# Ninth chunk's attention in four array quarters, and the last two tiles' stores merged, in a linear-attention-plus-MLP kernel

## Chip, cores and metric

The kernel runs on one core of one Trainium2 chip. The metric is the device time of one execution in microseconds (us). A core has these engines: TensorE (PE, with its weight loads shown apart as PEld), VectorE (DVE), ScalarE (ACT), GpSimd (POOL) and SyncE (SP). SP, ACT and POOL also issue DMA transfers. TensorE writes into PSUM, which has eight banks; VectorE and ScalarE read it from there.

## The reference

Inputs are q, k and v of shape (8, 8, 576, 64): batch, heads, sequence, head width. All inputs and the output are float32.

```python
q_s = softmax(q, axis=-1)                       # over the 64 features
k_s = softmax(k, axis=2)                        # over the sequence
kv = np.einsum('bhsd,bhse->bhde', k_s, v)       # 64 x 64 per head
attn = np.einsum('bhsd,bhde->bhse', q_s, kv)
x = attn.transpose(0, 2, 1, 3).reshape(8, 576, 512)
xn = (x - mean(x)) / sqrt(var(x) + 1e-6) * g_ln
out = x + relu(xn @ w_ch1) @ w_ch2              # 512 -> 2048 -> 512
```

## The kernel before

**Chunks and tiles.** The 576 rows of each batch are cut into 512 and 64. The 512 rows are a chunk of 4 tiles of 128 rows, so there are eight chunks, 0 to 7, one for each batch. The eight remainders of 64 rows make a ninth chunk, `C9`: its tile `t` holds in partitions 0 to 63 the remainder of batch `2t`, in partitions 64 to 127 that of batch `2t + 1`.

**Attention of a chunk.** For each pair of heads `i` (4 pairs of 2 x 64 = 128 features), `kv_sb[:, b, i, :]` holds a 128x128 block with the two heads' 64x64 matrices on its diagonal and zeros elsewhere. `po_mm` (line 380) multiplies the transposed exponentials of q, `eqTs`, with it. For chunks 0 to 7 that is one matmul per tile and pair, over the full array (line 387). For the ninth chunk (line 394) the two halves of a tile belong to different batches, so each pair takes two matmuls: 128 rows of the array (both heads), 64 columns (the 64 tokens of one batch), and 128 streamed columns of that batch's block, half of whose products are with zeros. The two matmuls write partitions 0 to 63 and 64 to 127 of the same bank. A tile `po` (128 x 512 float32) fills one PSUM bank and comes from the pool `att_ps`, which has two banks; so tile 0 takes the first, tile 1 the second, tile 2 the first again and tile 3 the second again.

**After it.** `x_fast` (line 424) reads a bank on VectorE: one `scalar_tensor_tensor` (line 427) scales by the reciprocals of the softmax sums (`eqs[c][2]`, one for each head) and adds up the row (`accum_out`) into `mv[:, t, 0:1]`. `xn_out` (line 419) then centres the row. `square_sum` (line 407, ScalarE) adds up the squares. `xn_T` (line 267) transposes two tiles at a time by a DMA on SP's queue, and `sum_x` (line 259) makes the sums of transposed blocks that the next product needs.

**The MLP of a chunk.** Both products are done by a seven-product (Strassen-like) scheme. `mm1_fast` (line 714; matmuls of line 711, outputs `bx`, `bb`, `bc`) makes the hidden layer `hT`. `mm2_fast` (line 644; matmuls of line 566, banks `ba`, `bb`, `bc`, `be`) does the second product. VectorE (lines 550, 594, 742, 745) and ScalarE (lines 591, 666, 735, 739, 753) form the sums between the products. Line 577 makes the output tiles of chunks 1 to 7.

**What sets the order.** The program is written out by hand, in order, for every engine (`manual_schedule`). `run` (line 798) walks through a chunk's matmuls, each with a weight of 0.5, and puts the side work in where the running sum of weights passes a given number. While chunk 7's MLP runs, `attn_rest` (line 870) makes the ninth chunk's attention: tiles 0 and 1 at 14, their reads at 22 and 54, tiles 2 and 3 at 58, their reads at 66 and 75. Squares are at 46, 62, 69 and 77, the transposes at 61 and 78. So each engine meets this work at a fixed place in its queue.

**The end.** The last chunk's second product is `last_products` (line 596). Its outputs lie in one tile `yl`; `stt` (line 606, VectorE) writes one 128x256 half of one tile. `store` (line 611) issues two DMAs, partitions 0 to 63 from SP's queue and 64 to 127 from ACT's (line 616). There are five calls, so ten DMAs: three of two tiles (128 KB each) and two of one tile (64 KB each). After them SP waits for every DMA queue's semaphore, one by one (line 1147), and the program ends.

Of the kernel before, what the change touches and what calls it, by code (L numbers as in the profile page):

```python
# [12 lines left out]
FP32 = mybir.dt.float32  # L13
BF16 = mybir.dt.bfloat16
AF = mybir.ActivationFunctionType
ALU = mybir.AluOpType
# [4 lines left out]
def kernel(  # L21
# [16 lines left out]
    nc = tc.nc  # L38

    B, H, S, D = q.shape  # L40
    DM = H * D
    DH = 4 * DM
    P = 128
# [5 lines left out]
    NP = H // 2  # L49
# [3 lines left out]
    C9 = B  # L53
# [15 lines left out]
    att_ps = ctx.enter_context(tc.tile_pool(name="att_ps", bufs=2, space=PS))  # L69
# [19 lines left out]
    kv_sb = const.tile([P, B, NP, P], BF16)  # L89
# [85 lines left out]
    eks, eqs, eqTs, xs, xnTs, rstds, tqs = {}, {}, {}, {}, {}, {}, {}  # L175
# [165 lines left out]
    halves = (slice(0, 64), slice(64, P))  # L341
# [36 lines left out]
    pobox = {}  # L378

    def po_mm(c, t, i):  # L380


        if i == 0:
            pool, tag = (mm_ps, "m") if c == 0 and t >= 2 else (att_ps, "a")
            pobox["p"] = pobox[c, t] = pool.tile([P, DM], FP32, tag=tag, name="po")
        if c < B:
            nc.tensor.matmul(  # L387
                pobox["p"][:, i * P : i * P + P], eqTs[c][:, t, i, :], kv_sb[:, c, i, :],
                start=True, stop=True,
            )  # L390
        else:
            for half in range(2):
                ps = slice(64 * half, 64 * half + 64)
                nc.tensor.matmul(
                    pobox["p"][ps, i * P : i * P + P], eqTs[c][:, t, i, ps],
                    kv_sb[:, 2 * t + half, i, :], start=True, stop=True,
                )

    def stats(c, t, src):
        _, st, _, mv = xs[c]  # L400
# [15 lines left out]
    def xn_out(c, t):  # L416

        x, _, xn, mv = xs[c]
        nc.vector.tensor_scalar(
            out=xn[:, t], in0=x[:, t], scalar1=float(DM), scalar2=mv[:, t, 0:1],  # L420
            op0=ALU.mult, op1=ALU.subtract,
        )

    def x_fast(c, t):

        x, st, _, mv = xs[c]
        nc.vector.scalar_tensor_tensor(  # L427
            x[:, t].rearrange("p (h d) -> p h d", h=H),
            in0=pobox[c, t].rearrange("p (h d) -> p h d", h=H), scalar=1.0,
            in1=eqs[c][2][:, t].to_broadcast([P, H, D]), op0=ALU.mult, op1=ALU.mult,  # L430
            accum_out=mv[:, t, 0:1] if c else st[:, t, 0:1],
        )
        if c:
            xn_out(c, t)
# [35 lines left out]
    hbox = {}  # L470
# [68 lines left out]
    def sum_h(g, i):  # L539

        if g == 0 and i == 0:
            hbox["s"] = mlp.tile([P, 4, KH, 2 * P], BF16, tag="hs", name="hs", bufs=1)
        ks = slice(KH // 2 * g, KH // 2 * g + KH // 2)
        s1, s2, s3, s4 = [hbox["s"][:, n, ks] for n in range(4)]
        a11, a12, a21, a22 = [h_part(odd, half, ks) for half in range(2) for odd in range(2)]
        dst, x, y, op = (
            (s1, a21, a22, ALU.add), (s2, s1, a11, ALU.subtract),
            (s3, a11, a21, ALU.subtract), (s4, a12, s2, ALU.subtract),
        )[i]
        nc.vector.tensor_tensor(out=dst, in0=x, in1=y, op=op)  # L550
# [18 lines left out]
    def bank(name):  # L569
        hbox[name] = mm_ps.tile([P, 2, DH2], FP32, tag="m", name="b" + name)  # L570
# [18 lines left out]
    def copy_u(name):  # L589
        hbox[name] = mlp.tile([P, 2, DH2], FP32, tag=name, name=name, bufs=1)  # L590
        nc.scalar.copy(hbox[name], hbox["a"])  # L591

    def add_u(dst, src):
        nc.vector.tensor_tensor(out=hbox[dst], in0=hbox["b"], in1=hbox[src], op=ALU.add)

    def last_products(product):

        c = C9
        yl = raw.tile([P, T, DM], FP32, tag="qt", name="yl")

        def part(t, col):
            return yl[:, t, DH2 * col : DH2 * col + DH2]

        def stt(t, col, src, add=None):
            cols = slice(DH2 * col, DH2 * col + DH2)
            nc.vector.scalar_tensor_tensor(
                part(t, col), in0=src, scalar=rstds[c][:, t : t + 1],
                in1=xs[c][0][:, t, cols] if add is None else add, op0=ALU.mult, op1=ALU.add,
            )

        def store(t0, tn, col):
            cols = slice(DH2 * col, DH2 * col + DH2)
            for half, eng in enumerate((nc.sync, nc.scalar)):
                ps = slice(64 * half, 64 * half + 64)
                to = out[2 * t0 + half : 2 * (t0 + tn) - 1 + half : 2, SM:S, cols]
                eng.dma_start(to.transpose([1, 0, 2]), yl[ps, t0 : t0 + tn, cols])

        def both(name, t0, col, add=False):
            for t in range(2):
                stt(t0 + t, col, hbox[name][:, t], part(t0 + t, col) if add else None)  # L620

        def own_bank():
            bank("d")

        def seed_e():
            bank("e")
            add_u("e", "s2")

        product(1, "a", first=True, cut=6, at={
            0: [lambda: sum_h(1, 0), lambda: sum_h(1, 1)],  # L630
            15: [lambda: both("a", 0, 0)]})
        product(2, "c", first=True, at={7: [lambda g=g: sum_h(g, 2) for g in range(2)],
            15: [lambda: both("c", 0, 0, True), lambda: store(0, 2, 0)]})
        product(6, "a", at={7: [lambda g=g: sum_h(g, 3) for g in range(2)], 15: [lambda: copy_u("s2")]})
        product(5, "b", first=True)
        product(7, "a", at={1: [seed_e, lambda: both("b", 2, 1)], 15: [
            lambda: both("a", 2, 1, True), lambda: stt(3, 0, hbox["a"][:, 1]),
            lambda: store(2, 2, 1)]})
        product(3, "e", at={15: [lambda: both("e", 0, 1), lambda: store(0, 2, 1), own_bank]})
        product(4, "a", ts=(0,), at={7: [lambda: stt(2, 0, hbox["a"][:, 0]), lambda: store(2, 1, 0)]})  # L640
        product(4, "d", ts=(1,), own=True, at={
            15: [lambda: stt(3, 0, hbox["d"][:, 1], part(3, 0)), lambda: store(3, 1, 0)]})

    def mm2_fast(c):

# [26 lines left out]
        if c == C9:  # L672
            last_products(product)
            return steps
# [154 lines left out]
    def attn_fast(c):  # L829

        s = [(4 + 4 * t, lambda t=t: reduce_q(3, t, 2)) for t in (0, 2)] if c == 3 else []
        kv, new, ps, squares, ts, rstd = (
            (24, 40, ((48, 53), (57, 59), (65, 67), (73, 75)), (66, 74, 87, 91), (61, 78), 95)
            if c == 3 else
            (3, 10, ((13, 24), (48, 53), (57, 59), (65, 67)), (60, 66, 74, 87), (55, 70), 92)
        )
        s += [(22 if c == 3 else 2, lambda: recip_q(c)), (kv, lambda: kv_pairs(c)), (new, lambda: start_x(c))]
        for t, (p0, p1) in enumerate(ps):
            s += spread([lambda t=t, i=i: po_mm(c, t, i) for i in range(NP)], p0, p1)
            s += [(p1, lambda t=t: x_fast(c, t)), (squares[t], lambda t=t: square_sum(c, t))]  # L840
        s += [(ts[0], lambda: xn_T(c, 0, 2)), (ts[1], lambda: xn_T(c, 2, 2)), (rstd, lambda: rstd_op(c))]
        s += [((84, 100 if c == C9 - 1 else 88, 92, 101)[i], lambda i=i: sum_x(c, i)) for i in range(4)]
        return s
# [26 lines left out]
    def attn_rest():  # L870

        s = [(2, lambda: recip_q(C9)), (4, lambda: start_x(C9))]
        for t, (p0, p1, p2) in enumerate(((14, 22, 46), (14, 54, 62), (58, 66, 69), (58, 75, 77))):
            s += [(p0, lambda t=t: [po_mm(C9, t, i) for i in range(NP)])]
            s += [(p1, lambda t=t: x_fast(C9, t)), (p2, lambda t=t: square_sum(C9, t))]
        s += [(61, lambda: xn_T(C9, 0, 2)), (78, lambda: xn_T(C9, 2, 2)), (88, lambda: rstd_op(C9))]
        return s + spread([lambda i=i: sum_x(C9, i) for i in range(4)], 102, 104)
# [274 lines left out]
```

## Time and profile before

| what | value |
|---|---|
| median of three runs | 264.89 us (264.72 to 265.26) |
| the profiled execution itself | 264.57 us |
| its span, first to last instruction | 262.8 us |
| granted TensorE clock, mean | 0.998 |
| line 394, ninth chunk's attention matmuls | 32, in two visits of 16, from 211.1 and 221.4 us |
| line 427, read of a 512-wide tile on VectorE | 0.68 us, and 0.08 us to read the accumulator |
| line 407, squares of a tile on ScalarE | 0.72 us, and 0.20 us to read the accumulator |
| last VectorE instruction (line 606) | starts at 258.45 us, takes 0.48 |
| end stores | 128 KB: 2.5 us (SP) and 2.8 us (ACT) from issue to landing |

A row of the timeline has the start (us from the start of the span), the time that the row covers, the engine, the line, the operation, what is written from what, the shape and the count; in brackets stands how long the engine had been idle before and what ended that. For matmuls the shape begins with the used part of the array (rows * columns), and a matmul's time is its whole way through the array, so matmuls overlap: their cost is read from the distances of their starts. A page line with shares of the chain follows the work back from the last instruction, at each step to what released it.

### The profile page before, as it was taken

How to read it: one execution, taken by the hardware profiler on the slowest of the kernel's cores; microseconds unless marked ns; L12 is line 12 of the kernel's file. 1: busy time of each engine (PE TensorE's matmuls, PEld its weight loads, DVE VectorE, ACT ScalarE, POOL GpSimd, SP SyncE). 2: the span in 40 equal slices, each digit the busy share in tenths (PEclk: the TensorE clock that was granted, in tenths of full speed). 3: DMA queues.
4: the chain of work that ended last, by engine and by line, in shares of the span. 5: the costliest groups of instructions: out<-in, count | busy, mean ns of one | idle time of the engine just before them, and what ended most of it. 6: DMA issues, size and time to landing. Idle time of an engine off the chain costs nothing.

```text
span 262.8 us, 6694 instructions
## 1 busy us (share of the span) xinstructions
PE 255.6 (97%) x2624; PEld 220.0 (84%) x2627; DVE 224.0 (85%) x492; ACT 174.3 (66%) x340; POOL 94.8 (36%) x148
## 2 busy tenths in 40 slices
PE   8999989999999999999999999999999999999993
PEld 6789745789888898999899889998899888888882
DVE  6879597999999999899889988998898869977872
ACT  4557780888977885789478947894788378447400
POOL 3962228233079104930980097009000800030000
PEclk9999999999999999999999999999999999999999
DMA  6999999979958995999299929994906320321014
GB/s 193 254 205 206 356 218 283 282 185 298 170 125 265 281 140 67 284 274 129 67 301 247 167 62 278 247 169 94 266 5 127 115 81 10 73 102 60 2 41 120
DMA packets 82536, 45.00 MB, mean 171 GB/s; under 512 B 58116, under 2 KB 79112, under 8 KB 82504
## 3 DMA queue, kind: packets, MB, share of 16 engines
q0 software_dynamic: 32464, 21.76, 44.2%
q1 hardware_dynamic: 49440, 22.29, 39.0%
q10 hardware_dynamic: 600, 0.53, 0.6%
q8 instruction: 20, 0.33, 0.5%
q14 instruction: 12, 0.10, 0.1%
HBM read 36.70 MB, written 9.44 MB: 176 GB/s over the span
## 4 chain that ended last, share of the span: by engine, by line
PE 82%; DMA 9%; POOL 3%; DVE 3%; ACT 1%; issue 0%; DVEq 0%
PE ba L566 21%; PE bx L711 20%; PE bb L711 10%; DMA qt<-in_q_dram 9%; PE be L566 5%; PE bc L566 5%; PE bb L566 5%; PE bc L711 5%; PE pc L519 3%; PE po L387 2%; PE pkv L357 2%; PE ph L483 1%; DVE x L427 1%; POOL w_raw L99 1%; DVE ot L500 1%; POOL v L965 1%
## 5 line engine op out<-in xcount | busy, mean ns | idle before, releaser
L566 PEld LDWEIGHTS <-hs 128*128 128x128 bf16 x512 | 49.8, 98 | 5.7
L711 PEld LDWEIGHTS <-w_q 128*128 128x128 bf16 x480 | 45.6, 98 | 5.1
L259 POOL TENSOR_TENSOR tq<-xnT 128x256 bf16<-128x256 bf16 x26 | 17.2, 677 | 77.0 <-DMA xnT<-xn 63.0
L566 PEld LDWEIGHTS <-hT 128*128 128x128 bf16 x384 | 37.1, 98 | 4.3
L711 PEld LDWEIGHTS <-w1g 128*128 128x128 bf16 x360 | 34.1, 98 | 4.1
L711 PE MATMUL bx<-tq,w_q 128*128 128x256 bf16 x240 | 31.7, 273 | 0.0
L566 PE MATMUL ba<-w_q,hs 128*128 128x256 bf16 x256 | 30.8, 273 | 0.0
L735 ACT COPY bc<-bx 128x512 f32<-128x512 f32 x30 | 16.7, 591 | 20.8 <-PE bx L711 20.5
L742 DVE TENSOR_TENSOR bb<-bx,s 128x512 f32<-128x512 f32 x30 | 19.5, 695 | 8.4 <-ACT s L739 5.7
L583 POOL DMA_DIRECT2D out_dram<-ot x28 | 15.4, 558 | 24.2 <-DVE ot L577 24.1
L427 DVE SCALAR_TENSOR_TENSOR x<-po,rq 128x512 bf16<-128x512 f32 x34 | 23.2, 683 | 0.9 <-PE po L387 0.7
L407 ACT ACTIVATE scrap<-x,mv 128x512 bf16<-128x512 bf16 x32 | 23.0, 720 | 1.4 <-DVE x L427 1.2
L753 ACT ACTIVATE hT<-bb 128x512 bf16<-128x512 f32 x30 | 16.3, 595 | 9.9 <-PE bb L711 9.1
L745 DVE TENSOR_TENSOR hT<-bx,s 128x512 bf16<-128x512 f32 x30 | 19.3, 684 | 3.8 <-PE bx L711 3.8
L387 PE MATMUL po<-kv_sb,eqT 128*128 128x128 bf16 x128 | 22.1, 219 | 0.0
L550 DVE TENSOR_TENSOR hs<-hT 128x1024 bf16<-128x1024 bf16 x32 | 21.6, 685 | 0.5 <-ACT hT L753 0.5
L753 ACT ACTIVATE hT<-bc 128x512 bf16<-128x512 f32 x30 | 16.4, 595 | 8.4 <-PE bc L711 8.4
L218 DVE TENSOR_REDUCE zq<-eq 128x16 f32<-128x1024 bf16 (+1 forms) x20 | 20.7, 1051 | 0.0
L591 ACT COPY s<-ba 128x512 f32<-128x512 f32 x15 | 8.7, 582 | 13.3 <-PE ba L566 8.6
L753 ACT ACTIVATE hT<-bx 128x512 bf16<-128x512 f32 x30 | 16.4, 604 | 0.7 <-PE bx L711 0.7
L566 PE MATMUL ba<-w_sb,hT 128*128 128x256 bf16 x128 | 16.7, 273 | 0.0
L739 ACT COPY s<-bb 128x512 f32<-128x512 f32 x30 | 16.5, 619 | 0.0
(152 smaller groups left out, 550.3 us busy)
## 6 DMA issues: line engine op xcount, KB each, us to landing
out_dram<-ot POOLq DMA_DIRECT2D x30, 256.0 KB, 5.0
qt<-in_q_dram SPq DMA_DIRECT2D x5, 1024.0 KB, 6.7
kt<-in_k_dram SPq DMA_DIRECT2D x5, 1024.0 KB, 12.2
qt<-in_q_dram POOLq DMA_DIRECT2D x2, 1024.0 KB, 12.4
kt<-in_k_dram POOLq DMA_DIRECT2D x2, 1024.0 KB, 14.1
vm<-in_v_dram POOLq DMA_DIRECT2D x16, 128.0 KB, 12.6
w_raw<-in_moe_w_ch_dram POOLq DMA_DIRECT2D x3, 512.0 KB, 10.4
w_sb<-in_moe_w_ch_dram POOLq DMA_DIRECT2D x3, 512.0 KB, 16.2
```

What stands on the lines that cost most here:

```text
L218: nc.vector.reduce_sum(eqs[c][1][:, ts], eqs[c][0][:, ts], axis=AX.X)
L259: eng.tensor_tensor(out=dst[:, t], in0=x[:, t], in1=y[:, t], op=ALU.subtract)
L387: nc.tensor.matmul(pobox["p"][:, i * P : i * P + P], eqTs[c][:, t, i, :], kv_sb[:, c, i, :], start=True, stop=True,)
L407: nc.scalar.activation(scrap, x[:, t], AF.Square, bias=mv[:, t, 0:1], scale=-float(DM), accum_out=mv[:, t, 1:2],)
L427: nc.vector.scalar_tensor_tensor(x[:, t].rearrange("p (h d) -> p h d", h=H), in0=pobox[c, t].rearrange("p (h d) -> p h d", h=H), scalar=1. ...
L550: nc.vector.tensor_tensor(out=dst, in0=x, in1=y, op=op)
L566: nc.tensor.matmul(hbox[bank][:, t], lhsT, rhs, start=first and (own or t == 0) and k == 0, stop=k == KH - 1, skip_group_check=True)
L711: nc.tensor.matmul(dst[:, q], lhsT, rhs, start=first and q == 0 and ko == 0, stop=ko == 1, skip_group_check=True)
L735: nc.scalar.copy(at[g, "c"], at[g, "x"])
L742: nc.vector.tensor_tensor(out=at[g, "b"], in0=at[g, "x"], in1=at[g, "s"], op=ALU.add)
L745: nc.vector.tensor_tensor(out=h_out(g, 1, 1), in0=at[g, "x"], in1=at[g, "s"], op=ALU.add)
L753: nc.scalar.activation(h_out(g, odd, half), at[g, name], AF.Relu)
```

## The change

For the ninth chunk, `po_mm` takes two banks for each pair of tiles (`t` = 0 and 1, then 2 and 3) and does four matmuls for each tile and pair of heads: batch `m` of the tile by head `half` of the pair. Each has 64 rows (one head's features), 64 columns (one batch's tokens) and 64 streamed columns (that head's 64x64 matrix). Rows 0 to 63 of the array (the first head) write the first bank, rows 64 to 127 (the second head) the second one. A visit (two tiles) is then 32 matmuls instead of 16. `x_fast` reads a tile with two `scalar_tensor_tensor` of 4 x 64 columns, one from each bank, with a row sum each, and a `tensor_add` of 128x1 joins the two sums. Chunks 0 to 7 keep their code. At the end, the store of tile 2's left half is left out, and the last call stores tiles 2 and 3 together: four calls, eight DMAs of 128 KB.

```diff
     def po_mm(c, t, i):
+        if c == C9:
+            if i == 0 and t % 2 == 0:
+                pobox["q"] = [
+                    att_ps.tile([P, 2, NP, D], FP32, tag="a", name="po") for _ in range(2)
+                ]
+            pobox[c, t] = pobox["q"]
+            for m, tok in enumerate(halves):
+                for half, hs in enumerate(halves):
+                    nc.tensor.matmul(
+                        pobox["q"][half][tok, t % 2, i, :], eqTs[c][hs, t, i, tok],
+                        kv_sb[hs, 2 * t + m, i, hs], start=(t % 2 == 0 and i == 0), stop=True,
+                        skip_group_check=True,
+                    )
+            return
         if i == 0:
             ...
-        if c < B:
-            nc.tensor.matmul(
-                pobox["p"][:, i * P : i * P + P], eqTs[c][:, t, i, :], kv_sb[:, c, i, :],
-                start=True, stop=True,
-            )
-        else:
-            for half in range(2):
-                ps = slice(64 * half, 64 * half + 64)
-                nc.tensor.matmul(
-                    pobox["p"][ps, i * P : i * P + P], eqTs[c][:, t, i, ps],
-                    kv_sb[:, 2 * t + half, i, :], start=True, stop=True,
-                )
+        nc.tensor.matmul(
+            pobox["p"][:, i * P : i * P + P], eqTs[c][:, t, i, :], kv_sb[:, c, i, :],
+            start=True, stop=True,
+        )
...
     def x_fast(c, t):
         x, st, _, mv = xs[c]
+        if c == C9:
+            for half in range(2):
+                nc.vector.scalar_tensor_tensor(
+                    x[:, t].rearrange("p (i two d) -> p i two d", two=2, d=D)[:, :, half],
+                    in0=pobox[c, t][half][:, t % 2], scalar=1.0,
+                    in1=eqs[c][2][:, t].rearrange("p (i two) -> p i two", two=2)[:, :, half]
+                    .to_broadcast([P, NP, D]),
+                    op0=ALU.mult, op1=ALU.mult, accum_out=st[:, t, half : half + 1],
+                )
+            nc.vector.tensor_add(mv[:, t, 0:1], st[:, t, 0:1], st[:, t, 1:2])
+            xn_out(c, t)
+            return
...
-        product(4, "a", ts=(0,), at={7: [lambda: stt(2, 0, hbox["a"][:, 0]), lambda: store(2, 1, 0)]})
+        product(4, "a", ts=(0,), at={7: [lambda: stt(2, 0, hbox["a"][:, 0])]})
         product(4, "d", ts=(1,), own=True, at={
-            15: [lambda: stt(3, 0, hbox["d"][:, 1], part(3, 0)), lambda: store(3, 1, 0)]})
+            15: [lambda: stt(3, 0, hbox["d"][:, 1], part(3, 0)), lambda: store(2, 2, 0)]})
```

## The prediction

> **What bounds the kernel now.** I read the page first: the busy shares, then the chain that ended last.
>
> ```profile
> PE 255.6 (97%) x2624; PEld 220.0 (84%) x2627; DVE 224.0 (85%) x492; ACT 174.3 (66%) x340; POOL 94.8 (36%) x148
> ...
> PE 82%; DMA 9%; POOL 3%; DVE 3%; ACT 1%; issue 0%; DVEq 0%
> ```
>
> TensorE (PE) is busy for 97% of the span, and it makes up 82% of the chain. Other engines matter where they hold PE up. The granted clock is 0.998, so no term below has a clock in it. Then I read the timeline around the two places where the ninth chunk's attention (line 394) stands.
>
> ```profile
> 210.62 0.60 PE L711 MATMUL bc<-xnT,w1g 128*128 128x256 bf16 x4
> 211.15 0.64 PE L394 MATMUL po<-kv_sb,eqT 128*64 128x128 bf16 x16
> 211.72 0.61 PE L711 MATMUL bc<-xnT,w1g 128*128 128x256 bf16 x4
> ```
>
> ```profile
> 220.71 0.68 DVE L427 SCALAR_TENSOR_TENSOR x<-po,rq 128x512 bf16<-128x512 f32 x1
> ...
> 221.32 0.08 DVE L427 DVE_READ_ACCUMULATOR x<-po,rq 128x1 f32 x1
> ...
> 221.43 0.64 PE L394 MATMUL po<-kv_sb,eqT 128*64 128x128 bf16 x16
> ```
>
> Full-array matmuls start 109 ns apart. The four at 210.62 leave PE free at 211.06, and the next of their kind starts at 211.72: a visit of line 394 costs 0.66 us. The second costs the same: four of line 566 start at 220.90, PE is free at 221.34, and the next starts at 222.00. Ahead of it DVE reads tile 1 from its bank, from 220.71 to 221.40; part 2 comes back to that. In the single records, 16 matmuls start as 8 pairs, 3 to 4 ns apart within a pair and 56 ns from pair to pair (80 before the second): 8 x 56 = 448 ns. The other 0.21 us is the way into the half array and back.
>
> **Part 1, the quarters.** Each visit's 16 matmuls of 128 rows x 64 columns (128 streamed) become 32 of 64 x 64 (64 streamed), with as many weight loads. Four in a row use four different quarters. If they run at once, a visit is 8 groups of four at a pitch P, plus the same 0.21 us. No row shows quarters. The nearest row for P is line 357, two half-array tiles with 65 streamed columns:
>
> ```profile
> 182.53 0.32 PE L357 MATMUL pkv<-vm,ek 128*64 128x65 bf16 x8
> ...
> 183.16 0.20 PE L357 MATMUL pkv<-vr,ekr 128*64 128x65 bf16 x2
> 183.29 0.39 PE L711 MATMUL bx<-xnT,w1g 128*128 128x256 bf16 x2
> ```
>
> Its 40 matmuls are 20 pairs. The first starts at 182.53, the last at 183.16: 0.63 / 19 = 33 ns a pair, and 32 without the slower first step. That visit costs 0.85 us, 20 x 32 = 0.64 and again 0.21, so the cost of going in and out does not hang on the count. I take P = 32: 64 streamed columns instead of 65, and the partner tiles ride 4 ns behind. That is 256 ns against 448, **0.19 us less a visit, 0.38 for two**. Bounds for P: 29 ns, the shorter steps of line 357, gives 0.43; above, a group that splits into two pairs, 64 ns, costs 0.13 for two visits, and four matmuls one by one are the second rival. I take the low end because halves side by side already overlap in this trace.
>
> **Part 2, the banks, a wait that is added.** Before, tiles 0 to 3 alternated between two banks, and only the 9th matmul of the second visit (tile 3, at 221.68) needed the read of tile 1, over at 221.40. After, every tile lies in both banks, and the first two matmuls of the second visit wait for tile 1's two reads. All of PE's later matmuls are queued behind the second one. When does that read end? An accumulating read of 512 columns holds DVE 0.61 us up to its 0.08 us accumulator read; one of 128 (line 312) 0.27; one of 256 lies at about 0.39, which is also the step of the 256-wide line 606. The second read starts 0.39 to 0.51 after the first (accumulator read overlapped, or waited for as before line 419, 0.12), so it is done 0.39 + 0.39 + 0.08 = 0.86 to 0.98 us after 220.71: 221.58 to 221.70, and PE sees it some 0.05 later. PE would have started its second matmul at 221.43. **The wait is 0.20 to 0.32 us; I take 0.22**, since line 891 at 17.79 starts with the accumulator read ahead of it still running. Does DVE come earlier? Its chain from 217.25 to 221.40 has no idle, and hangs on ScalarE's copies and through them on PE's bank bb at 213.64, after the first visit; it moves forward with PE. DVE's added time on tile 0 (at 214.47) ends in an idle of 1.10 us ahead of 217.25. So the wait stands, and gives back more than the second visit gains.
>
> **Part 3, DVE.** Per tile, one read (0.73 us to the start of line 419) becomes two reads, two accumulator reads and a 128x1 add: 0.90 to 1.02 up to the add, which with its own wait takes 0.18 (line 445's 0.14 plus 0.04), so +0.35 to +0.48; I take 0.38. The add could be hidden (+0.30), not below. DVE runs without idle from 220.71 to 227.5, so tiles 1 to 3 add up. The cover is in these lines:
>
> ```profile
> 227.01 0.59 ACT L591 COPY s<-ba 128x512 f32<-128x512 f32 x1 [0.17 <-PE ba L566]
> ...
> 228.76 0.88 DVE L577 SCALAR_TENSOR_TENSOR ot<-bc,rstd,x 128x256 f32<-128x256 f32 x2 [0.43 <-PE bc L566]
> ...
> 231.12 0.70 DVE L594 TENSOR_TENSOR bb<-bb,s 128x512 f32<-128x512 f32 x1 [0.69 <-ACT s L591]
> ```
>
> The 1.14 us of delay, less the 0.2 for which line 594 (227.63, 0.70) had waited, arrives there as 0.95; PE's product 3 needs its bank at 230.31, 1.97 after it was ready. The idles of 0.43 and 0.69 swallow the rest: by 231.12 DVE is on time with 0.26 to spare. ScalarE is closer: tile 3's squares (226.03) must wait for its read and start near 226.99; the copy of line 591 behind them ends near 228.29 instead of 227.60, and product 7 needs it at 228.56. Spare 0.27; with +0.48 a tile it is missed by 0.1. The transposes on SP's queue land about 1.2 us later, at 228.8; their reader at 229.55 now comes at 229.98. I cost part 3 at 0.
>
> **Part 4, the stores.** SP and ACT each issue four stores instead of five; tile 2's left half now leaves with tile 3's. SP's last issue starts at 258.97, set by DVE's last read (258.45 + 0.48), and still will. ACT's last started at 259.25, kept by its previous issue of 0.82; now 258.97.
>
> ```profile
> out_dram<-yl SPq DMA_DIRECT2D x3, 128.0 KB, 2.5
> out_dram<-yl ACTq DMA_DIRECT2D x3, 128.0 KB, 2.8
> out_dram<-yl SPq DMA_DIRECT2D x2, 64.0 KB, 2.3
> out_dram<-yl ACTq DMA_DIRECT2D x2, 64.0 KB, 2.8
> ```
>
> Before, the last landing was ACT's at 261.50 (2.24 after issue; the 2.8 is the other one's). After: SP 258.97 + 2.47 = 261.44, ACT 258.97 + 2.77 = 261.74. At the end SP waits for the stores' semaphores one after the other, 62 ns each. Before, ACT's last stood third of nine, and six steps followed it, to 261.88. After, SP's last stands second: 261.45 plus seven steps is 261.88, and ACT's stands ninth, long enough behind to be in by then (261.76). Same end: **0**, between -0.1 (both land a little sooner) and +0.24 (the later landing is paid in full).
>
> **Sum.** -0.38 + 0.22 + 0 + 0 = -0.16 us. The profiled execution took 264.57 us (span 262.8 and 1.8 around it); so 264.41 by its measure. The median of the three runs is 0.32 above it, 264.89, and I put the forecast there: **264.73 us**. 0.2% is 0.53 us, about what a measurement of this kernel can tell from no change.
>
> **Rivals.**
> - *PE isn't held by the read* (10%): DVE comes sooner than I work out, and both visits gain: -0.38, 264.51. For it: the time of a 256-wide accumulating read is interpolated, not shown. Against it, even at 0.34 a read the second bank is free at 221.47, still after 221.43, and there is no idle on DVE ahead of the read.
> - *Quarters are issued one by one* (8%), slower than before: small full-array matmuls start no closer than 25 ns (line 296, one column: 18 in 0.59 us, less one's 0.164, over 17). 32 x 25 = 0.80 us a visit instead of 0.448: +0.70 for two, with the wait +0.92, 265.81. It decides from P = 42 ns up (16 P = 0.896 - 0.22); over 0.2% slower from P = 75. Against it: pairs 3 to 4 ns apart in lines 357 and 394. The Trainium skill's page "TensorE: Matmul & The Clock Gate" (section "Wait — 56ns, not 53.3ns?") states this floor as a rule, about 25 ns from start to start however small the matmul; line 296 agrees, line 357 doesn't. The same page (section "Part 3: Packing small matmuls — row/col tiling") has tiles start about 4 ns apart, by which P would be near 30; for row halves no run here shows it.
> - *Only pairs overlap* (14%): P = 64, +0.13 + 0.22 = +0.35, 265.24. For it: 64 weight loads and matmuls a visit, 4 ns each at P = 32, where line 357 shows 8 ns (4 in 32).
> - *The later landing is paid* (10%): +0.24 - 0.16 = +0.08, 264.97. For it: ACT's 128 KB always took 2.77 to 2.79.
> - *DVE's extra time reaches PE at product 7* (6%): +0.1 to 0.2 on the forecast, about 264.9.
>
> The forecast has the other 52%. Range: from the first rival at its best P (-0.43) less the 0.17 us by which the runs fell under their median, 264.3, to the pairs case plus 0.2, 265.4; outside are the one-by-one case and some 8% of edges. Faster by over 0.53 us is in no case but an edge: 0.02. Slower: one by one and the worst of the pairs, 0.10. The same: 0.88.
>
> **What would show it.** Right: visits of line 391 (its number in the changed kernel) of about 0.47 us and 0.7 (with an idle on DVE ahead of its second matmul); four starts in some 12 ns, then 32; DVE's reads at 0.39 to 0.48 us; line 594 near 228.6 relative to PE; no PE idle at product 7; ACT's last landing near 261.7 with SP's chain ending as before. Wrong: a pitch of 42 ns or more, a longer way in and out than 0.21 us, or an end that follows ACT's landing.

## The result, and the profile after

| | median, us | runs | lowest to highest |
|---|---|---|---|
| kernel before | 264.65 | 22 | 264.26 to 265.26 |
| changed kernel | 265.52 | 22 | 264.08 to 268.24 |

The changed kernel is slower: ratio 1.0032, 95% interval [1.0016, 1.0047]. The forecast was 264.73 us with a range of 264.3 to 265.4 and 0.88 on no change, so time and sign are both missed. The spread says as much as the median: the best run is 0.18 us below the best of before, but the highest that counts lies 2.2 us above the highest of before (267.44; the 268.24 is a slow run and is left out of the ratio). That 267.44 is the profiled execution of the changed kernel (span 265.5), so its trace shows a long one.

Line numbers of the changed kernel stand 18 above those of before where no other line is named (711 is now 729, 577 is 595, 594 is 612, 566 is 584); line 391 holds the quarter matmuls, 435 the two reads, 442 the add. First the page, its busy line and its chain:

```profile
PE 255.7 (96%) x2659; PEld 219.5 (83%) x2659; DVE 223.9 (84%) x504; ACT 174.7 (66%) x340; POOL 94.1 (35%) x148
...
PE 9%; DVE 0%; issue 0%
```

PE is as busy as before, in a span 2.7 us longer. The chain can be followed back over only 9% of the span, so it doesn't tell the cause, and I asked by stages. Columns of these rows: window, its length, then busy time (and instructions) of PE, PEld, DVE, ACT and POOL, granted clock, DMA share, GB/s. The changed kernel, then the kernel before:

```profile
74.00:84.00 10.00, 8.82 (x98) 7.46 (x97) 8.20 (x18) 5.42 (x11) 6.53 (x11) 1.00 1.09 235
84.00:210.00 126.00, 126.00 (x1348) 112.81 (x1343) 112.71 (x234) 92.28 (x183) 53.79 (x82) 1.00 0.95 171
210.00:225.00 15.00, 15.00 (x194) 13.08 (x193) 12.08 (x32) 12.16 (x25) 1.09 (x3) 1.00 0.22 78
225.00:241.00 16.00, 14.62 (x134) 12.79 (x132) 12.00 (x35) 6.66 (x15) 2.14 (x4) 1.00 0.33 94
```

```profile
74.00:84.00 10.00, 10.00 (x126) 8.83 (x124) 9.55 (x20) 6.19 (x12) 9.87 (x15) 1.00 0.61 167
...
225.00:241.00 16.00, 16.00 (x149) 14.34 (x147) 12.77 (x31) 7.72 (x17) 2.14 (x4) 1.00 0.27 83
```

PE lost time in two places: at 74 to 84 us, where the code is the same as before, and at 225 to 241 us, behind the ninth chunk's attention. The attention itself, on PE's timeline of the changed kernel:

```profile
211.98 0.60 PE L729 MATMUL bc<-xnT,w1g 128*128 128x256 bf16 x4
212.51 0.45 PE L391 MATMUL po<-kv_sb,eqT 64*64 64x64 bf16 x32
212.89 0.61 PE L729 MATMUL bc<-xnT,w1g 128*128 128x256 bf16 x4
...
222.07 0.60 PE L584 MATMUL ba<-w_sb,hT 128*128 128x256 bf16 x4
222.60 0.55 PE L391 MATMUL po<-kv_sb,eqT 64*64 64x64 bf16 x32
223.08 1.48 PE L584 MATMUL ba<-w_sb,hT 128*128 128x256 bf16 x12
```

Four matmuls from 211.98 leave PE free at 212.42, the next starts at 212.89: the visit costs 0.47 us instead of 0.66. The second costs 0.57 (222.51 to 223.08). The attention gained what it was to gain. Now the place where PE lost it, in the timeline of DVE and PE, the changed kernel and then the kernel before:

```profile
233.19 0.49 DVE L259 TENSOR_TENSOR tq<-xnT 128x256 bf16<-128x256 bf16 x2 [2.29 <-issue]
...
237.11 0.60 PE L729 MATMUL bb<-tq,w_q 128*128 128x256 bf16 x4 [1.19 <-DVE ot L595]
...
237.90 0.60 PE L729 MATMUL bb<-tq,w_q 128*128 128x256 bf16 x4 [0.19 <-DVE ot L595]
```

```profile
229.55 0.49 DVE L259 TENSOR_TENSOR tq<-xnT 128x256 bf16<-128x256 bf16 x2
...
234.67 1.04 PE L711 MATMUL bb<-tq,w_q 128*128 128x256 bf16 x8
```

DVE stands idle for 2.29 us ahead of `sum_x` (line 259), which reads what the second DMA transpose of the ninth chunk writes; in the trace of before it started at 229.55 with no idle. Everything behind it on DVE is late, down to the output reads of line 595, and PE waits for the bank that these free. The DMA view of 226 to 234 us of this run (queue and kind: packets, MB, share; then issues: KB, us to landing):

```profile
q1 hardware_dynamic: 1056, 0.26, 17.7%
q8 instruction: 1, 0.02, 0.7%
...
xnT<-xn SPq DMA_TRANSPOSE x1, 4.8
```

The transpose, issued at 228.34, landed 4.8 us later; before, the two landed 3.04 and 3.05 us after their issue (221.94 and 226.35). Of its sixteen pieces, fifteen were in after 3.04 to 3.18 us. In the single DMA records, the transpose's last 256-byte packet ends at 231.098; at 231.094 a packet of 16,384 bytes on queue q8 (kind "instruction") starts and takes 0.93 us; the transpose's last two 4-byte packets come at 232.009, as it ends. There are 20 such fetches in the span, one to some 260 of PE's 5,300 instructions (matmuls and weight loads), and 21 in e5 below, which adds 64 instructions on PE: so I take them for PE's instruction blocks. Before, the nearest one started at 232.09, well behind that landing at 229.40.

**Theory A**, before the experiments: two movements of the change meet. DVE's longer reads issue the transpose later, and 64 more PE instructions (32 matmuls and their weight loads) bring the fetch sooner; the fetch delays one piece, DVE waits in order, PE waits for DVE. Below, a trace in which one piece is late has a *meeting*; the others *escaped*. **Rivals:** the late transpose alone does it (C), the merged stores (D), jitter of the DMAs that the change has no part in (E).

### The profile page after: what moved, and what is told of

Its sections match the earlier page's. It is cut to its first block, busy times and chain, and to the rows that moved or that the text cites. A ratio compares the mean times of both kernels' runs of the same rounds, so it can differ in the third digit from the quotient of the medians.

```text
span 265.5 us, 6769 instructions
## 1 busy us (share of the span) xinstructions
PE 255.7 (96%) x2659; PEld 219.5 (83%) x2659; DVE 223.9 (84%) x504; ACT 174.7 (66%) x340; POOL 94.1 (35%) x148
## 5 line engine op out<-in xcount | busy, mean ns | idle before, releaser
L445 DVE SCALAR_TENSOR_TENSOR x<-po,rq 128x512 bf16<-128x512 f32 x30 | 20.5, 684 | 1.0 <-PE po L400 0.8
L729 PE MATMUL bb<-tq,w_q 128*128 128x256 bf16 x120 | 15.7, 272 | 2.3 <-DVE ot L595 1.4
```

The source lines that it names most:

```text
L445: nc.vector.scalar_tensor_tensor(x[:, t].rearrange("p (h d) -> p h d", h=H), in0=pobox[c, t].rearrange("p (h d) -> p h d", h=H), scalar=1. ...
L729: nc.tensor.matmul(dst[:, q], lhsT, rhs, start=first and q == 0 and ko == 0, stop=ko == 1, skip_group_check=True)
```

## The experiments

The start of the program differs from execution to execution by more than the effect: loads arrive sooner or later. To read a trace in spite of that, I took the start of every ACTIVATE and COPY on ScalarE (301 in each kernel) less that of the same instruction in the trace of before. From 100 to 208 us that offset is constant to 0.02 us in every trace; so "last part" below is the offset of the last of them (at 251.6 us in the trace of before), less the offset at 208, in us. Landing and fetch are counted from the issue of the second transpose.

| trace | offset at 208 | last part | landing | fetch starts |
|---|---|---|---|---|
| changed kernel | +1.37 | **+1.40** | 4.77 | 2.75 |
| e1 changed again | +1.83 | -0.30 | 3.05 | 2.60 |
| e12 changed, third | -0.27 | -0.30 | 3.03 | 2.56 |
| e2 quarters only | +1.35 | **+1.40** | 4.77 | 2.75 |
| e3 cut read | +0.61 | 0.00 | 3.04 | 5.47 |
| e4 stores only | +0.64 | -0.02 | 3.03 | 5.85 |
| e5 changed, padded | +0.61 | -0.29 | 3.04 | before the issue |
| e6, e11, e15 before, padded | +0.67, -0.49, +1.55 | -0.02 to 0.00 | 3.03 to 3.04 | 2.51 to 2.57 |
| e7 cut read, padded | -0.47 | **+1.52** | 4.68 | 2.66 |
| e8 earlier read | +0.11 | -0.29 | 3.04 | 2.75 |
| e9 earlier read, padded | -0.02 | -0.29 | 3.02 | before the issue |
| e10, e16 changed, short warm-up | -0.50, +0.43 | -0.30 | 3.04 | 3.15, 3.01 |
| e13 before, short warm-up | +0.43 | 0.00 | 3.03 | 7.43 |
| e14 earlier read, short warm-up | -0.49 | -0.30 | 3.03 | 4.19 |

### e1 and e12: the changed kernel again

No edit.

> The changed kernel once more, for a second trace. Theory A (two movements that meet: DVE's +0.27 us a tile sends the second transpose of the ninth chunk about 1.2 us later relative to PE, and 64 more PE instructions bring PE's next instruction fetch earlier; the fetch holds back one of the transpose's sixteen pieces by about 1.6 us, DVE waits for it in order, and PE waits at bank bb of line 729): ratio to before 1.001 to 1.005, DVE idle over 1.5 us ahead of line 259 near 233 and PE idle over 1 us ahead of line 729 near 237, in the trace again, while the extra 1.5 us near 78 us, where the code is the same, may or may not come again. Rival E (DMA jitter that the change has no part in): the idle near 237 is gone, and the median lies within 0.2% of before. Either way the two attention visits cost 0.47 and 0.58 us.

> The changed kernel a third time, for one more trace. Theory A: either the fetch starts right behind the transpose's last packet and one piece lands some 4.8 us after the issue, and the part from 208 us to the end is 1.40 us longer than in the kernel before, or it escapes, and that part is 0.29 us shorter; nothing between.

e1: 264.93 us against 264.79 (35 runs of before on that chip), ratio 1.0019 [0.9993, 1.0045], runs up to 267.48. Its traced execution (266.35 us) escaped, and is long by its start alone (+1.83 at 208); e12's (264.12 us) escaped too. DVE's row in e12:

```profile
229.81 0.49 DVE L259 TENSOR_TENSOR tq<-xnT 128x256 bf16<-128x256 bf16 x2 [0.55 <-issue]
```

The idle is 0.55 us here, and PE shows no wait at all behind it. The last part is one of two values, -0.30 or +1.40, nothing between, as e12's expectation said, in these two traces and the first. In e1 the fetch started at 231.403, 4 ns after the transpose's last 4-byte packet was through (231.399). The extra 1.5 us at 74 to 84 us appears in no other trace of this study.

### e2 and e4: quarters without the merged stores, and the stores alone

```diff
-        product(4, "a", ts=(0,), at={7: [lambda: stt(2, 0, hbox["a"][:, 0])]})
+        product(4, "a", ts=(0,), at={7: [lambda: stt(2, 0, hbox["a"][:, 0]), lambda: store(2, 1, 0)]})
...
-            15: [lambda: stt(3, 0, hbox["d"][:, 1], part(3, 0)), lambda: store(2, 2, 0)]})
+            15: [lambda: stt(3, 0, hbox["d"][:, 1], part(3, 0)), lambda: store(3, 1, 0)]})
```

(e2, against the changed kernel; e4 has these two lines of the change in the kernel before.)

> The change without the merged stores (the old five calls). Theory A: the same late transpose and the same ratio as the changed kernel, 1.001 to 1.005, since the end costs nothing either way (within 0.1 us). Rival D (the merged stores cost the time): ratio 0.999 to 1.000, 0.5 to 0.9 us under the changed kernel.

> The kernel before with the merged stores alone. Prediction's part 4 and theory A: 0, between -0.1 and +0.1 us, landing to end unchanged at about 3.8 us after DVE's last instruction. Rival D: +0.5 us or more.

e2: 265.41 us, 1.0022 [1.0000, 1.0043], and the same late piece in its trace. e4: 264.64 us, 1.0002 [0.9986, 1.0018]. The merged stores cost nothing; rival D falls.

### e3: the cut read alone

In the kernel before, two reads and an add in place of line 427 (banks and matmuls as before):

```diff
+        if c == C9:
+            for half in range(2):
+                hh = slice(4 * half, 4 * half + 4)
+                nc.vector.scalar_tensor_tensor(
...
+                    op0=ALU.mult, op1=ALU.mult, accum_out=st[:, t, half : half + 1],
+                )
+            nc.vector.tensor_add(mv[:, t, 0:1], st[:, t, 0:1], st[:, t, 1:2])
```

> The kernel before, whose read of a tile is cut into two 256-wide reads and a 128x1 add: DVE's delay alone, with no instruction more on PE and the old banks. Theory A (the delay needs the moved instruction fetch to hurt): transposes land about 1 us later relative to PE than before, DVE idle ahead of line 259 up to 0.9 us, PE's idle ahead of line 711 near 236 at most 0.3 us, time +0.1 to +0.4 us (part of it PE's wait for tile 1's read is not there, since the banks are the old ones). Rival C (the late transposes alone cost it): PE idle over 1 us near 236 and +0.8 to +1.7 us, ratio 1.003 to 1.006. By the step of the prediction that put DVE's extra work at nothing: 0.

264.78 us, 1.0003 [0.9992, 1.0015], no run over 265.33. DVE's row:

```profile
230.89 0.49 DVE L259 TENSOR_TENSOR tq<-xnT 128x256 bf16<-128x256 bf16 x2 [0.56 <-issue]
```

DVE waits 0.56 us for the transpose, as in e12, and PE does not notice (last part 0.00). The late transpose alone is free here: rival C falls.

### e5, e6, e11, e15 and e7: the fetch moved sooner

More but shorter matmuls in the warm-up at the start, 32 more in all; in the changed kernel (e5), the kernel before (e6, and again e11 and e15) and the cut read (e7):

```diff
-        warm(34)
+        warm(27)
+        warm(39, 16)
```

> The changed kernel with 32 more matmuls in the warm-up at the start (27 of the old width and 39 of 16 columns instead of 34 of the old), which take about the same time there but move every later instruction fetch of PE some 64 instructions, about 3.5 us, earlier against the work: the fetch that met the transpose at 231.1 should come near 227.6, before the transpose's packets (229.5 to 231.1). Theory A (late transpose and moved fetch meet): the second transpose of the ninth chunk lands 3.0 to 3.1 us after its issue, no idle over 0.4 us ahead of line 729 near 237, and the time falls to 0.0 to 0.4 us under the kernel before (ratio 0.9985 to 1.0005), with no run over 266.3. Rival C (the late transpose by itself) and rival E (jitter of the DMAs): as the changed kernel, 1.001 to 1.004, with runs up to 267.

> The kernel before with the same 32 matmuls in the warm-up: its fetch of PE instructions, at 232.1 before, should come near 228.6, into the second transpose's flight (issued 226.35, packets 227.5 to 229.1, landed 229.4). Theory A: one piece of the transpose lands 0.7 to 1.7 us late in the trace (or only just escapes it), DVE idle ahead of line 259, PE waits 0.3 to 1.5 us near 236, ratio 1.001 to 1.005, with none of the change in the kernel. Rivals C and E: no change, ratio 0.9985 to 1.0015.

> The cut read (DVE's delay alone, 264.78 us and no change as it stood) with the same 32 matmuls in the warm-up: its fetch, at 233.24 as it stood, should come near 229.7, into the later transpose's flight (packets 228.9 to 230.35). Theory A: the late landing and PE's wait near 237 come back without a quarter matmul or a merged store: landing 4 to 4.8 us after issue, ratio 1.002 to 1.006, and more than the kernel before with the same padding, since here the transpose has no time to spare. Rival C: as the cut read, 1.000. Rival E: the same.

> The kernel before with the padded warm-up once more, for a second trace: its runs were 0.8 us longer than those of the kernel before, but the one execution in the trace had just escaped (fetch at 229.54, as the transpose's packets ended). Theory A: in most of its executions one piece lands late, and this one has an even chance or better to show it: landing 4 to 4.8 us after the issue, and 0.7 to 1.4 us more between 208 us and the end than in the kernel before. If it escapes again, the cause of its 0.8 us stays open.

> The kernel before with the padded warm-up, a repeat of a measurement of 1.0031 [1.001, 1.0052]. If the padding makes the fetch meet the transpose in a good part of its executions (theory A): 1.001 to 1.005 again; one late piece would cost some 0.8 us here, since the transpose is issued 1.2 us earlier against PE than in the changed kernel. If the first measurement was the start of the program (loads), as both of its traces suggest: 0.9985 to 1.0015.

e5: 264.45 us against 264.55, 0.9989 [0.9972, 1.0006], no run over 265.52; the fetch came at 225.46, before the transpose's issue, and the late piece is gone. DVE's row in e5:

```profile
230.70 0.49 DVE L259 TENSOR_TENSOR tq<-xnT 128x256 bf16<-128x256 bf16 x2 [0.56 <-issue]
```

e7: 266.23 us, 1.0060 [1.0036, 1.0083], no run under 265.49. There is no quarter matmul and no merged store in e7, and its trace shows the same picture; DVE's row, then PE's (lines 723 and 589 are 711 and 577 of the kernel before):

```profile
231.45 0.49 DVE L259 TENSOR_TENSOR tq<-xnT 128x256 bf16<-128x256 bf16 x2 [2.19 <-issue]
```

```profile
235.38 0.60 PE L723 MATMUL bb<-tq,w_q 128*128 128x256 bf16 x4 [1.01 <-DVE ot L589]
236.16 0.60 PE L723 MATMUL bb<-tq,w_q 128*128 128x256 bf16 x4 [0.19 <-DVE ot L589]
```

Here the fetch started at 229.361, at the end of the transpose's last 256-byte packet, and the last two 4-byte packets followed it at 230.28. So a fetch and a transpose that meet are enough, whatever made them meet.

e6 came out as expected in its time (265.55 us, 1.0031 [1.0010, 1.0052]) but not in its trace: the fetch started 2.52 us after the issue, as the transpose's packets ended, no piece was late, and the last part is as before. e11 escaped too, and e15 measured 1.0012 [0.9992, 1.0033], its traced execution long at the start (PE waits 2.5 us until 17.0 us). So a meeting in the kernel before is not shown, and why e6 measured 0.8 us more stays open: the padding can cost time ahead of the last part.

### e8, e9, e10, e16, e14 and e13: out of the meeting

The transpose sooner (e8; e9 with `warm(27)` and `warm(31, 16)` as well):

```diff
-        for t, (p0, p1, p2) in enumerate(((14, 22, 46), (14, 54, 62), (58, 66, 69), (58, 75, 77))):
+        for t, (p0, p1, p2) in enumerate(((14, 22, 46), (14, 54, 62), (58, 66, 69), (58, 67, 77))):
...
-        s += [(61, lambda: xn_T(C9, 0, 2)), (78, lambda: xn_T(C9, 2, 2)), (88, lambda: rstd_op(C9))]
+        s += [(61, lambda: xn_T(C9, 0, 2)), (70, lambda: xn_T(C9, 2, 2)), (88, lambda: rstd_op(C9))]
```

The fetch later, by 22 matmuls fewer (e10 and e16 the changed kernel, e13 the kernel before, e14 together with the edit of e8):

```diff
-    junk = const.tile([P, 256], BF16)
+    junk = const.tile([P, 512], BF16)
...
-        warm(34)
+        warm(17, 512)
...
-        warm(11)
+        warm(6, 512)
```

> The changed kernel with DVE's read of tile 3 at 67 instead of 75 and the transpose of tiles 2 and 3 at 70 instead of 78, so that the transpose is issued before the output reads of line 595 take DVE. Theory A: the transpose lands about 1 us earlier, ahead of the fetch, no wait near 237, and the 0.28 us that PE gains at the visits stay: ratio 0.998 to 1.000, runs of 264 to 265.3. If instead DVE's other work (line 595, line 612), moved behind the read, holds PE's banks, PE's waits move to lines 584 and 612 and the time rises by 0.2 to 0.5.

> The earlier read and transpose (the changed kernel with tile 3's read at 67 and the transpose at 70) with 24 more matmuls in the warm-up (27 wide ones and 31 of 16 columns for 34 wide ones), so that PE's instruction fetch, which stood 0.15 us behind the transpose's last piece there, comes near 226.1, before the transpose's packets (227.0 to 228.5). Theory A: the part from 208 us to the last ScalarE instruction is 0.29 us shorter than in the kernel before, no idle over 0.4 us ahead of line 729 near 236, ratio 0.997 to 0.9995, no run over 266. Rivals C and E: as the earlier read without the padding, with single runs near 267.

> The changed kernel with 22 matmuls fewer in the warm-up (17 and 6 of 512 columns for 34 and 11 of 256), so that PE's instruction fetch comes about 2.4 us later against the work, near 233.5, behind the transpose's landing at 231.4: the other way out of the meeting. Theory A: the transpose lands 3.05 us after its issue, the part from 208 us on is 0.29 us shorter than in the kernel before, ratio 0.998 to 1.0005, no run over 266.3. If the number of instructions or the late transpose itself cost the time: as the changed kernel, 1.002 to 1.003, with runs up to 267.

> The kernel before with the short warm-up (17 and 6 matmuls of 512 columns for 34 and 11 of 256). Its fetch moves from 232.1 to about 233 to 234.5, still clear of the transpose's landing at 229.4. Theory A: nothing to gain, ratio 0.9985 to 1.0015, and the changed kernel with the same warm-up is 0.2 to 0.5 us under it. Rival F (the short warm-up itself gives the time): ratio 0.9965 to 0.998, as the changed kernel with the short warm-up.

> The changed kernel with the earlier read of tile 3, the earlier transpose, and the short warm-up. Theory A: transpose lands 3.05 us after issue and before the fetch, the part from 208 us to the end 0.29 us shorter than in the kernel before, ratio 0.997 to 0.9995, no run over 266. Rival F: 0.996 to 0.998, and no better than the kernel before with the short warm-up.

> The changed kernel with the short warm-up, a repeat of 0.9972 [0.996, 0.9984]. Theory A: 0.997 to 0.9995 (0.29 us is 0.0011; the rest of the first measurement would be the start of the program), no run over 266, transposes landing 3.05 us after issue. Rival F: 0.996 to 0.998, and the same as the kernel before with the short warm-up.

| | median | before, same chip | ratio | highest run |
|---|---|---|---|---|
| e8 | 264.46 | 264.55 | 0.9997 [0.9974, 1.0021] | 267.08 |
| e9 | 264.36 | 264.72 | 0.9998 [0.9981, 1.0015] | 266.44 |
| e10 | 264.05 | 264.72 | 0.9972 [0.9960, 0.9984] | 264.20 |
| e16, the same | 264.12 | 264.72 | 0.9972 [0.9961, 0.9983] | 264.68 |
| e14 | 264.22 | 264.72 | 0.9974 [0.9961, 0.9987] | 264.75 |
| e13, before with the short warm-up | 264.22 | 264.72 | 0.9986 [0.9976, 0.9996] | 264.98 |

The ratios on record are not those of the two medians, as e9's row shows.

All of these traces of the changed kernel have the last part at -0.29 or -0.30. The DMA view of e10, 226 to 231 us:

```profile
q1 hardware_dynamic: 1056, 0.26, 27.9%
q8 instruction: 1, 0.02, 1.4%
...
xnT<-xn SPq DMA_TRANSPOSE x1, 3.0
```

The fetch lies in the same window again, but it starts at 229.62, 0.56 us behind the transpose's last 256-byte packet, and the landing is 3.0. That is out of the meeting, though not by the step that the expectation named: it had the fetch near 233.5, behind the landing. With the short warm-up none of 15 runs (e10, e16) is over 264.68, and this version is 0.28% under the kernel before in both measurements. It was not timed beside the changed kernel, but for e12's single execution on e10's chip, which escaped and took 264.12. Not all of the gain is the change (rival F, that the short warm-up itself gives the time, holds for about half): e13 shows about 0.4 us for the short warm-up by itself (0.0014 of 264.7), and the changed kernel adds another 0.0014, where the traces show 0.30 us (0.0011); the intervals of e13 and e16 overlap a little. Where the warm-up's share comes from isn't visible in the last part (0.00 in e13); it lies at the start, and I did not follow it. e8 and e9 keep some long runs (267.08, 266.44) that their traces don't explain; e9's expectation had none over 266.

## Why the prediction was wrong

**Part 1 was right.** Matmuls of a group of four start 3 to 4 ns apart and groups 31.8 ns, after a first step of 52; a visit without a wait costs 0.47 us. The two rivals on the pitch (one by one, only pairs) fall.

**Part 2 was right in kind and too dear.** The second visit's second matmul waited 0.11 us for tile 1's second read instead of 0.22, because that read followed the first after 0.34 us, not 0.39; so the rival by which PE isn't held falls too. Together the visits gain 0.19 + 0.09 = 0.28 us, and the last part shows -0.29 to -0.30 wherever the changed kernel escapes; the forecast had -0.16.

**Part 3 is the step that failed**, in the sentence "The transposes on SP's queue land about 1.2 us later, at 228.8" and in the cost of 0 drawn from it. Its size for DVE was somewhat high; DVE's timeline for tile 1 in the changed kernel:

```profile
221.89 0.42 DVE L435 SCALAR_TENSOR_TENSOR x<-po,rq 128x256 bf16<-128x256 f32 x1
222.23 0.08 DVE L435 DVE_READ_ACCUMULATOR x<-po,rq 128x1 f32 x1
222.23 0.42 DVE L435 SCALAR_TENSOR_TENSOR x<-po,rq 128x256 bf16<-128x256 f32 x1
222.57 0.08 DVE L435 DVE_READ_ACCUMULATOR x<-po,rq 128x1 f32 x1
222.69 0.16 DVE L442 TENSOR_TENSOR mv<-st 128x1 f32<-128x1 f32 x1
222.89 0.35 DVE L425 TENSOR_SCALAR xn<-x,mv 128x512 bf16<-128x512 bf16 x1
```

1.00 us to the row of line 425 instead of 0.73: +0.27 a tile (predicted 0.38). Three tiles make 0.81, and the 0.19 that the first visit gains comes off: by the clock of before, the second transpose is issued at 226.97 in every trace of the changed kernel that leaves it in its place, 0.62 us later than before and not 1.2. But I had also read the transpose's issue on SP (1.23 us) as the whole transfer. It lands 3.05 us after its issue starts; before, at 229.40, with its reader at 229.55. The spare that I put at over a microsecond was 0.15. That error alone would have cost nothing: the 0.62 less the 0.15 leaves a wait of about half a microsecond, and in e3 and in the five traces of the changed kernel without a meeting (e1, e5, e10, e12, e16) DVE waits some 0.55 us there and PE is on time: the cover that the prediction named (the idle of 0.69 ahead of line 594) swallows it. What the prediction had no term for, and so put at nothing, is a transfer that the change moves without issuing it: PE's own instruction fetch. I counted the 64 added PE instructions by their time on PE and not by what they do to the fetches. With DVE waiting in order for that landing and the fetch beside it, the meeting costs 1.40 + 0.30 = 1.70 us when it happens, and it happens in some executions: in two of the four traces whose code is the changed kernel's up to the end stores (the first, e1, e2, e12).

Line 594's first sum (612 now) came at 229.43, 1.17 of it the trace's offset at PE, so 228.3 by the clock of before (predicted 228.6), and cost nothing. **ScalarE at product 7** had 0.34 us to spare, as costed (0.27); that rival falls. **Part 4 was right**: e4 shows 0, and from DVE's last instruction to the end of the span is 3.76 us (261.72 to 265.48) instead of 3.80. The page's rows after:

```profile
out_dram<-yl SPq DMA_DIRECT2D x4, 128.0 KB, 2.4
out_dram<-yl ACTq DMA_DIRECT2D x4, 128.0 KB, 2.7
```

**How far it is settled.** That the meeting costs 1.5 us (e7) to 1.7 us, and that it needs both the later transpose and the fetch, is shown: by e3 (late transpose, fetch elsewhere: nothing), e7 (fetch moved to it: all of it), e5 and e10 (fetch moved off either way: gone). Half the executions at 1.70, less 0.30, would make the mean 0.55 us longer; the means stand 0.85 us (first chip, without the 268.24), 0.49 (e1) and 0.64 (e2) above before. That the half of four traces holds for all runs is an estimate, and the start adds its part: the offsets at 208 us differ by over 2 us, and the first trace has its own loss of 1.5 us near 78 us.

Which side an execution falls on is decided within some 0.2 us. In the three traces with a meeting the fetch started 2.66 to 2.75 us after the issue, at the end of the transpose's last 256-byte packet. That packet itself was late in them: it ended at 2.67 to 2.76 us, and by 2.59 in the fifteen other traces. So one of the sixteen pieces was 0.1 to 0.2 us behind before the fetch began; whether the fetch caused that too is not shown. Five fetches that started at 2.51 to 2.60 held nothing back, although in four of them the transpose's last packets followed within 0.1 us; e8's, also at 2.75, came after a transpose whose packets were done at 2.59. The records don't say which of the sixteen DMA engines a packet ran on. So rival E holds this much: chance picks the side. But the change is what brings the two so close; before, the fetch started 2.7 us after the landing.

The Trainium skill describes the two halves. The Trainium skill's page "Runtime: NRT & Kernel Launch" (section "Instruction fetch mechanics") has instructions come in blocks of 16 KiB, 256 instructions, over a DMA queue of the sequencer's own, a cost "mostly hidden"; the packets here are of that size, and took 0.93 us in the meetings, but in these one was not hidden. The Trainium skill's page "DMA: Bandwidth & Descriptors" (section "Queues, rings and completion order") says that a semaphore's write lands only after every earlier write of that DMA engine, across its queues; the two 4-byte packets that came as the fetch ended, in all three traces with a meeting, fit it, though the records don't say what these packets write, and a plain queue behind the fetch would look the same.

## What to carry to other kernels

Count a DMA's spare time from its landing to its reader, not from the end of its issue, and look hardest where an in-order engine reads it. When a change adds or removes instructions on the engine that sets the pace, it moves that engine's instruction fetches too (32 matmuls at the start put the fetch from 2.6 us behind the transpose's issue to 2.1 us ahead of it): find them in the DMA view, and see which transfer in need of its last piece lies next to one. When a changed kernel's best run is better and its median worse, look for something that happens in some executions only; a second trace is worth more than a finer median.

## What was not expected of the hardware

- With one 16 KB instruction block in front of its last two 4-byte packets, one of a transpose's sixteen pieces landed 1.6 us behind the other fifteen, though the block took 0.93 us itself. Part of it is that this piece was already up to 0.2 us behind; and from its last packet to its landing it took 1.06 us, where escaped ones take 0.45. Nothing here explains that last part.
- The fetch keeps near the end of a transpose's packets: with 22 matmuls fewer it came only 0.4 us later against the transpose (2.56 to 2.75 us after the issue, then 3.01 and 3.15) in the changed kernel, but 1.7 us later in the kernel before (5.75, then 7.43), where no transpose was in flight. It looks as if it had waited for the packets in the changed kernel; that is argued, not shown.
- On DVE an accumulating read starts at once beside the accumulator read of the one ahead (0.344 us from start to start for 256 columns, 0.42 us long each).
